# A gated FFT-and-MLP mixer on one core: first transfers regrouped, an earlier table load, two statistics on ScalarE, and a newly planned order

## Chip, core and metric

The kernel runs on one core of a Trainium2 chip. The metric is the device time of one execution in microseconds. It was timed three times: 136.17, 136.16 and 137.24 us, median 136.17. A further execution was profiled; the profile is of that one.

## What is computed

A token sequence `x` of 2048 rows by 512 columns goes through two branches, and a gate of each row mixes them:

```python
x = A_x
g = sigmoid((x * gate_w).sum(-1, keepdims=True))
# branch a: global filter in the frequency domain
X = rfft2(x.astype(float32)) * (A_w_r + 1j * A_w_i)
a = irfft2(X, s=(2048, 512)).astype(bfloat16)
# branch b: token-mixing MLP on the transposed, normalised input
h = layernorm(B_x)                                   # over the 512 columns
u = gelu(einsum("bsd,sf->bdf", h, B_w1) + B_b1)      # 2048 -> 1792
b = (einsum("bdf,fs->bds", u, B_w2) + B_b2).transpose(0, 2, 1)
return g * a + (1 - g) * b
```

The kernel reads `A_x` for both branches. Inputs and output are bfloat16.

## The kernel before, in words

**Tiling.** Row `512 q + 4 a + r` sits on partition `a`, in slot `(q, r)`, so there are 16 row tiles `j = 4 q + r` of 128 x 512. A "block" is one `r`: the four tiles `j = r, 4 + r, 8 + r, 12 + r`. Block 0 takes its tiles in the order j = 0, 8, 4, 12.

**Branch b.** VectorE (DVE) makes mean and variance of a tile (`bn_stats` L473, `bn_aggr` L474), ScalarE (ACT) the square root (L483), DVE reciprocal and -mean/std (L487, L488); the normalised tile `h` is written by ACT (L497), for j = 0, 4, 8 by DVE (L491). TensorE (PE) multiplies `h` with `w1` (L670, 14 x 16 matmuls, "m1"), ACT applies gelu (L684), PE multiplies with `w2` (L966, "m2"), ACT scales (L972) and DVE adds the other branch (L978); the last two tiles are finished by DVE alone (L984) before the stores.

**Branch a.** The 2D FFT is split into radix-4 butterflies on DVE and DFT matmuls on PE. In order: butterflies of `x` per block (L505 to L512); DFT matmuls `fa` (L524 to L527) with ACT copies L530; butterflies L537 to L544; a forward radix-4 step (`radix4`, L563 to L576) once for lt = 1 and once for lt = 0, the two halves of the frequencies, the second closed by a small copy L614; DFT matmuls `fb` (L632 to L635), eight groups for each half, each copied out by ACT (L639); column 0 is picked up by `c0a` (L754, L755) and multiplied in `c0b` (L772 to L777). Then DVE alone filters: `bfly` (L783, L784), products with the filter `W` (L791), `comb` (L796, L797), `ob` (L803 to L805), the inverse radix-4 (L563 to L579), all for lt = 0 and lt = 1. PE does the inverse DFT `i1` (L852 to L859), DVE joins (L875 to L888), PE does `i3` (L926 to L930), ACT scales by the gate (L937), DVE folds and adds (L949 to L953, L978).

**The filter's load.** `ld_W(comp)` issues 18 transfers on SyncE's (SP's) queue for the real part `A_w_r` and 18 for the imaginary part `A_w_i`, in rows of 514 bytes. `wprep` (L740, L743, L744) halves one row of `W` and adds the end columns of both parts (`wpm`, used by `c0b`). It reads both parts, so it can run only when the last filter transfers of `A_w_i` have landed.

**The order of the work.** Everything is added as a task with an engine, an estimated duration, what it reads and writes, and a priority. `Plan.order` plays the tasks through: whenever an engine is free, the ready task with the lowest priority number goes next. The emission order of the tasks is the program order of each engine, and on the chip each engine then runs strictly in that order, waiting where an input is late. So the planner's durations never cost time themselves; they only decide the order. A transfer's end is estimated from a rate (`RATE`, L132). `ld_W` is entered with 9.0 us of SP for the real part and 7.0 us for the imaginary one (L446).

**Names for the prediction's steps.** `ASTAT`, `XQ` and `here` come with the change; `PQ0` is the priority of block 0's butterflies; `HACT` the tiles normalised by ACT; `biasT`/`biasev` (L644 to L654) turn the biases to columns, which the gelu needs. PSUM has tags `fa` and `fb` with two buffers each, `acc` with four.

Of the kernel before, what the change touches and what calls it, by code (L numbers as in the profile page):

```python
# [16 lines left out]
P = 128  # L17
S = 2048
D = 512
# [109 lines left out]
    return {"flip": bf(np.eye(P)[::-1]), "ta": bf(ta), "ti": bf(ti), "tb": bf(tb), "tg": bf(tg)}  # L129


RATE = lambda t: 300e3 if t < 2.6 else 225e3 if t < 5.9 else 380e3  # L132


class Task:
# [3 lines left out]
class Plan:  # L139
# [32 lines left out]
    def order(self):  # L172
        for n, t in enumerate(self.tasks):
            t.left = len(t.deps)
            for d in t.deps:
                d.users.append(t)
        caps = dict(self.caps)
        pending = {}
        key = {t: (t.prio, n) for n, t in enumerate(self.tasks)}
        for t in self.tasks:  # L180
            if not t.left:
                pending.setdefault(t.eng, []).append(t)
        clock = {}
        dma_free = 0.0
        events = [(0.0, 0, None)]
        seq = 1
        out = []
        n_done = 0
        while events:
            now = events[0][0]  # L190
            while events and events[0][0] <= now + 1e-9:
                _, _, t = heapq.heappop(events)
                if isinstance(t, Task):
                    n_done += 1
                    for f in t.free:
                        caps[f] += 1
                    for u in t.users:
                        u.left -= 1
                        lat = self.SAME.get(u.eng, 0.0) if u.eng == t.eng else self.LAT
                        u.ready = max(u.ready, now + lat)  # L200
                        if not u.left:
                            pending.setdefault(u.eng, []).append(u)
                            heapq.heappush(events, (u.ready, seq, None))
                            seq += 1
            progress = True
            while progress:
                progress = False
                for eng, ts in pending.items():
                    if clock.get(eng, 0.0) > now + 1e-9:
                        continue  # L210
                    best = None
                    for t in ts:
                        if t.ready <= now + 1e-9 and all(caps[a] > 0 for a in t.alloc):
                            if best is None or key[t] < key[best]:
                                best = t
                    if best is None:
                        continue
                    ts.remove(best)
                    for a in best.alloc:
                        caps[a] -= 1  # L220
                    out.append((now, len(out), best))
                    clock[eng] = now + best.dur
                    end = now + best.dur
                    if best.nbytes:
                        dma_free = max(dma_free, now + best.dur + 1.0) + best.nbytes / RATE(dma_free)
                        end = dma_free + 0.9
                        clock[eng] = max(clock[eng], dma_free - 5.0)
                    best.end = end
                    heapq.heappush(events, (clock[eng], seq, None))
                    heapq.heappush(events, (end, seq + 1, best))  # L230
                    seq += 2
                    progress = True
        assert n_done == len(self.tasks), (n_done, len(self.tasks))
        self.total = max(t.end for t in self.tasks)
        return [t for _, _, t in out]
# [28 lines left out]
def kernel(  # L264
# [97 lines left out]


    Q0 = (0, 2, 1, 3)
    for r in range(4):
        if r == 0:
            for n, q in enumerate(Q0):
                ld([("x", 0, q)], lambda q=q: t["x"][:, q, 0, :], x4[:, q, 0, :], 131072, -9 + 0.1 * n, "SP" if n % 2 == 0 else "ACT")
        else:
            ld([("x", r, q) for q in range(4)], lambda r=r: t["x"][:, :, r, :], x4[:, :, r, :], 524288, 2 * r - (3 if r == 1 else 0))  # L370
        ld([("ta", r)], lambda r=r: t["ta"][:, r, :], tabs["ta"][:, r, :], 163840, 2 * r + 0.2 if r else -3.5)
# [16 lines left out]
    HI, LO, ALL = slice(P // 2, P), slice(0, P // 2), slice(0, P)  # L388
    w1_0(0, 0, LO, "ACT", -8)
    w1_0(1, 0, HI, "SP", -8)  # L390
    w1_0(0, 2, ALL, "ACT", -4)
    w1_0(0, 1, ALL, "SP", -4)
    w1_0(0, 3, ALL, "ACT", -3)
    for r in range(1, 4):
        add("SP", 0.5, ld_w1(r), writes=[("w1", 0, 4 * q + r) for q in range(4)], prio=2 * r + 0.5, nbytes=1024 * FA)
    load("flip", [P, P], BF16, tabs["flip"], 32768, prio=7)
# [57 lines left out]


    HACT = set(range(NJ)) - {0, 8, 4}
    PQ0 = 1.1
    for r in range(4):
        xk = [("x", r, q) for q in range(4)]
        groups = [[q] for q in Q0] if r == 0 else [[0, 1], [2, 3]]  # L460
        t["xf", r] = None
        for b, qs in enumerate(groups):
            js = [4 * q + r for q in qs]
# [7 lines left out]
            for j in js:  # L471
                def bn(j=j):
                    V.bn_stats(out=t["stats"][:, j, :], in_=t["x"][:, j // 4, j % 4, :])  # L473
                    V.bn_aggr(out=t["mv"][:, j, :], in_=t["stats"][:, j, :])  # L474
                add("DVE", d1(512) + 0.12, bn, reads=[("x", r, j // 4)], writes=[("mv", j)], prio=1.2 * r - (0.6 if r == 0 else 0))
# [6 lines left out]
            def sq(colv=colv, mvv=mvv):  # L482
                A.activation(colv("rstd"), mvv(1), ActF.Sqrt, bias=t["eps"][:, 0:1], scale=1.0)  # L483
            add("ACT", 0.25, sq, reads=mvk + ["eps"], writes=[("rstd", *g)], prio=-1)

            def rec(colv=colv, mvv=mvv, js=js):
                V.reciprocal(colv("rstd"), colv("rstd"))  # L487
                V.scalar_tensor_tensor(colv("nmr"), mvv(0), -1.0, colv("rstd"), op0=Alu.mult, op1=Alu.mult)  # L488
                for j in js:
                    if j not in HACT:  # L490
                        V.tensor_scalar(t["h"][:, j // 4, j % 4, :], t["x"][:, j // 4, j % 4, :], t["mv"][:, j, 0:1],  # L491
                                        t["rstd"][:, j:j + 1], op0=Alu.subtract, op1=Alu.mult)
            own = [j for j in js if j not in HACT]
            add("DVE", 0.25 + 0.32 * len(own), rec, reads=xb + mvk, writes=[("rstd", *g)] + [("h", j) for j in own], prio=1.2 * r - (0.2 if r else 0.9))
            for j in js:
                if j in HACT:
                    add("ACT", act(512, 2), lambda j=j: A.activation(t["h"][:, j // 4, j % 4, :], t["x"][:, j // 4, j % 4, :], ActF.Identity,  # L497
                                                                  bias=t["nmr"][:, j:j + 1], scale=t["rstd"][:, j:j + 1]),
                        reads=xb + [("rstd", *g)] + mvk, writes=[("h", j)], prio=-0.5 + 0.1 * r)

# [143 lines left out]
    def biasT():  # L644
        pb = t["pbias"] = ps([P, 32], F32, "fa", 2)
        T.matmul(pb[:, 0:NFT], lhsT=t["b1b"][:], rhs=t["flip"][:, P - NFT:P], start=True, stop=True)
        for r in range(4):
            T.matmul(pb[:, 16 + 4 * r:20 + 4 * r], lhsT=t["b2b"][:, r::4], rhs=t["flip"][:, P - 4:P], start=True, stop=True)
    add("PE", 0.3, biasT, reads=["bias", "flip"], writes=["pbias"], prio=9, alloc=["fa"])

    def biasev():
        V.tensor_copy(t["b1f"][:], t["pbias"][:, NFT - 1::-1])
# [20 lines left out]
    order = [(ft, j) for c in range(6) for j in jorder[2 * c:2 * c + 2] for ft in range(NF)]  # L673
    order += [(ft, j) for ft in range(NF) for j in jorder[12:]]
    order += [(ft, j) for ft in range(NF, NFT) for j in jorder]
    gelus = []
    m1t = []
    for n, (ft, j) in enumerate(order):
        last = j == jorder[-1]
        bank = bankof(ft)  # L680
        m1t.append(add("PE", mm(512), lambda ft=ft, j=j: m1(ft, j), reads=[("w1", w1of(ft), j), ("h", j)] + ([("w1", 0, j, n) for n in range(2)] if j % 4 == 0 else []), writes=[("u", ft)],
                       prio=10 + n * 1e-3, alloc=[bank] if j == jorder[0] else (), free={NF - 1: ["wa"], NF + 3: ["wb"], NFT - 1: ["wb"]}.get(ft, ()) if last else ()))
        if last:
            gelus.append(add("ACT", act(512, 1), lambda ft=ft: A.activation(  # L684
                t["gl"][:, ft, :], t["u", ft][:], ActF.Gelu_apprx_tanh, bias=t["b1f"][:, ft:ft + 1], scale=1.0),
                reads=[("u", ft), "b1f"], writes=[("gl", ft)] + ([("xf", (ft - 6) // 4)] if ft >= 6 else []), prio=0.5,
                free=[bank]))


# [1 line left out]
    for r in range(4):  # L691
# [4 lines left out]
        for q in range(4):  # L696
            def ga(q=q, r=r):
                A.activation(t["x"][:, q, r, :], t["x"][:, q, r, :], ActF.Copy, accum_out=t["glog"][:, 4 * q + r:4 * q + r + 1])  # L698
            gates.append(add("ACT", act(512) + 0.1, ga, reads=xk, writes=[("xg", q, r)], prio=5))
# [329 lines left out]
```

## Time and profile before

| | us |
|---|---|
| median of three timed runs | 136.17 |
| the profiled execution's own time | 135.25 |
| its span in the profile | 133.1 |
| PE busy | 125.3 (94% of the span) |
| DVE busy | 112.4 (84%) |
| ACT busy | 80.4 (60%) |
| first m1 matmul (L670) starts | 6.61 |
| last DVE instruction (L984) ends | 130.77 |

The granted TensorE clock is 1.0 throughout. The span is 2.15 us shorter than the execution's own time; what lies around the span is taken as unchanged. Matmuls of 128 x 512 are pipelined: one record lasts 0.38 us, but they start 0.216 us apart (28 of L670 take 6.42 us from first start to last end). Times below are from the start of the span.

### The profile page before, as it was taken

What the parts mean: (1) busy time and instruction counts of PE and PEld (TensorE: products, weight loads), DVE (VectorE), ACT (ScalarE), POOL (GpSimd) and SP (SyncE); (2) the same over time, 40 slices, a digit from 0 to 9 for tenths busy, and PEclk for the clock granted to TensorE, in tenths of its full rate; (3) what the DMA queues carried; (4) which work ended last, traced back from release to release, by engine and by line L of the source; (5) the groups of instructions that cost most, each with busy time, mean ns of one, the idle gap of its engine ahead of it and who ended that gap; (6) DMA issues with size and microseconds to landing.
All of it is one profiled execution on the core that took longest, in us unless ns stands there. A gap on an engine that the chain in (4) does not pass through costs nothing.

```text
span 133.1 us, 2156 instructions
## 1 busy us (share of the span) xinstructions
PE 125.3 (94%) x766; PEld 70.6 (53%) x780; DVE 112.4 (84%) x252; ACT 80.4 (60%) x157; POOL 0.2 (0%) x4
## 2 busy tenths in 40 slices
PE   6699899999799999999999999999999999999991
PEld 2245454545354475844445554556675665665591
DVE  2999999999969997359999999999777587979671
ACT  3344989975999999994222053332997557385500
POOL 0000000000000000000000000000000000000000
PEclk9999999999999999999999999999999999999999
DMA  4999999945499468899964800000000002130331
GB/s 148 263 381 389 395 390 385 371 88 128 92 259 285 93 152 273 271 415 402 412 246 145 330 0 0 2 5 2 0 0 0 5 0 106 52 158 5 158 118 40
DMA packets 17510, 23.18 MB, mean 174 GB/s; under 512 B 1606, under 2 KB 14940, under 8 KB 17500
## 3 DMA queue, kind: packets, MB, share of 16 engines
q1 hardware_dynamic: 16844, 22.21, 49.2%
q10 hardware_dynamic: 656, 0.84, 2.0%
q8 instruction: 6, 0.10, 0.3%
q14 instruction: 4, 0.03, 0.1%
HBM read 20.93 MB, written 2.10 MB: 173 GB/s over the span
## 4 chain that ended last, share of the span: by engine, by line
DVE 53%; PE 26%; ACT 13%; issue 4%; DMA 2%; DVEq 0%; ACTq 0%
PE acc L966 12%; DVE stats L473 7%; PE acc L670 4%; DVE xp L791 3%; DVE st L791 3%; ACT x L698 3%; ACT eo L937 3%; DVE st L564 3%; DVE mv L474 2%; DMA x<-in_A_x_dram 2%; ACT gl L684 2%; DVE xp L796 2%; DVE xp L563 2%; DVE B L803 2%; DVE xp L797 2%
## 5 line engine op out<-in xcount | busy, mean ns | idle before, releaser
L966 PE MATMUL acc<-gl,wa 128*128 128x512 bf16 (+1 forms) x107 | 26.9, 372 | 0.2
L966 PE MATMUL acc<-gl,wb 128*128 128x512 bf16 (+1 forms) x110 | 27.1, 372 | 0.1
L670 PE MATMUL acc<-h,wb 128*128 128x512 bf16 x108 | 25.7, 379 | 0.2
L972 ACT ACTIVATE x<-acc,ombb,omg 128x512 bf16<-128x512 f32 x14 | 10.8, 778 | 19.2 <-PE acc L966 19.1
L966 PEld LDWEIGHTS <-wa 128*128 128x128 bf16 x126 | 13.4, 114 | 9.8 <-issue 0.2
L966 PEld LDWEIGHTS <-wb 128*128 128x128 bf16 x126 | 13.4, 114 | 9.4
L670 PE MATMUL acc<-h,wa 128*128 128x512 bf16 x62 | 17.0, 379 | 1.5 <-DMA wa<-in_B_w_dram 1.0
L670 PEld LDWEIGHTS <-wb 128*128 128x128 bf16 x112 | 10.9, 98 | 11.7
L670 PEld LDWEIGHTS <-wa 128*128 128x128 bf16 x112 | 10.1, 98 | 10.7 <-DMA wa<-in_B_w_dram 1.8
L530 ACT CAST X<-fa 128x512 bf16<-128x512 f32 x16 | 9.3, 578 | 5.1 <-PE fa L527 5.1
L684 ACT ACTIVATE gl<-acc,b1f 128x512 bf16<-128x512 f32 x11 | 7.6, 694 | 7.8 <-PE acc L670 7.7
L473 DVE BATCH_NORM_STATS2 stats<-x 128x6 f32<-128x512 bf16 x16 | 10.8, 673 | 1.5 <-DMA x<-in_A_x_dram 1.5
L497 ACT ACTIVATE h<-x,nmr,rstd 128x512 bf16<-128x512 bf16 x13 | 10.0, 807 | 0.8 <-DVE nmr L488 0.8
L698 ACT ACTIVATE x<-x 128x512 bf16<-128x512 bf16 x16 | 10.0, 638 | 0.0
L670 PE MATMUL fb<-h,wa 128*128 128x512 bf16 x32 | 9.3, 379 | 0.1
L937 ACT ACTIVATE eo<-fa,g 128x512 bf16<-128x512 f32 x8 | 5.5, 688 | 6.1 <-DVE x L978 5.6
L355 PE MATMUL fa<-xp 128*128 128x512 bf16 x10 | 4.4, 623 | 1.2 <-DVE xp L316 1.2
L524 PE MATMUL fa<-rot,gl 128*128 128x256 bf16 x16 | 4.3, 271 | 1.2 <-ACT X L530 1.1
L937 ACT ACTIVATE eo<-fb,g 128x512 bf16<-128x512 f32 x8 | 5.5, 687 | 0.0
L670 PE MATMUL fa<-h,wa 128*128 128x512 bf16 x15 | 5.4, 379 | 0.0
L483 ACT ACTIVATE rstd<-mv,eps 128x2 f32<-128x2 f32 (+1 forms) x10 | 3.0, 295 | 3.4 <-DVE mv L474 2.8
L639 ACT CAST B<-fb 128x512 bf16<-128x512 f32 x8 | 4.9, 611 | 0.0
(172 smaller groups left out, 228.8 us busy)
## 6 DMA issues: line engine op xcount, KB each, us to landing
wb<-in_B_w_dram SPq DMA_DIRECT2D x11, 512.0 KB
wa<-in_B_w_dram SPq DMA_DIRECT2D x7, 512.0 KB
wa<-in_B_w_dram SPq DMA_DIRECT2D x3, 896.0 KB
x<-in_A_x_dram SPq DMA_DIRECT2D x3, 512.0 KB
wb<-in_B_w_dram SPq DMA_DIRECT2D x4, 384.0 KB
out_dram<-x SPq DMA_DIRECT2D x3, 512.0 KB
rot<-dft_ti SPq DMA_DIRECT2D x1, 736.5 KB
rot<-dft_ta SPq DMA_DIRECT2D x4, 160.0 KB
```

The lines of the kernel that those rows point to most:

```text
L355: T.matmul(pw[:], lhsT=t["warm"][:, 0:P], rhs=t["warm"], start=True, stop=True)
L473: V.bn_stats(out=t["stats"][:, j, :], in_=t["x"][:, j // 4, j % 4, :])
L497: add("ACT", act(512, 2), lambda j=j: A.activation(t["h"][:, j // 4, j % 4, :], t["x"][:, j // 4, j % 4, :], ActF.Identity, bias=t["nmr"][ ...
L530: add("ACT", act(512), lambda r=r, dq=dq: A.copy(t["X"][:, :, r, :, dq, :], t["pa", r, dq][:]), reads=[("pa", r, dq)], writes=[("X", r, dq ...
L639: A.copy(t["B"][:, lt, e, 2 * c:2 * c + 2, :].rearrange("p s (i b) -> p s i b", b=4), t["pb", lt, e, c][:].rearrange("p s b i -> p s i b"))
L670: T.matmul(t["u", ft][:], lhsT=w[:, j // 4, j % 4, c * P:(c + 1) * P], rhs=t["h"][:, j // 4, j % 4, :], start=(j == jorder[0]), stop=(j == ...
L684: gelus.append(add("ACT", act(512, 1), lambda ft=ft: A.activation(t["gl"][:, ft, :], t["u", ft][:], ActF.Gelu_apprx_tanh, bias=t["b1f"][:, ...
L698: A.activation(t["x"][:, q, r, :], t["x"][:, q, r, :], ActF.Copy, accum_out=t["glog"][:, 4 * q + r:4 * q + r + 1])
L791: V.tensor_mul(o, xs, w)
L937: A.activation(t["eo", j // 2][:, j % 2], t["i3", j][:], ActF.Copy, scale=t["g"][:, j:j + 1])
L966: T.matmul(t["y", j, n][:, cs], lhsT=w[:, o, 512 * q + r:512 * q + 512:4], rhs=t["gl"][:, ft, cs], start=(ft == 0), stop=(ft == NFT - 1))
L972: A.activation(tbuf(j).rearrange("p h d -> p (h d)"), t["y", j, 0][:], ActF.Identity, bias=t["ombb2"][:, j:j + 1], scale=t["omg"][:, j:j + 1])
```

## The change

The planner's transfer model gets another rate and a window of eight outstanding transfers per landing; some estimated durations are replaced; and these parts of the program change:

- Block 0 of `x` is loaded by three transfers on SP (j = 0; j = 8; j = 4 and 12 together) instead of four on SP and ACT; the first `w1` pieces (q = 0 and q = 2, 224 KB each, q = 0 no longer cut in halves) go first on ACT's queue, q = 1 and q = 3 on SP.
- Mean and variance of tiles j = 8 and j = 12 are made on ACT by two activations with accumulated sums each, into -mean and 512 x variance; the later steps of these tiles use them so.
- A tiny gelu activation (of one column) with priority 4.9, reading all `rstd`, so that the gelu table is loaded there and not at the first real gelu.
- `biasT` goes from priority 9 to -1; `PQ0` from 1.1 to -0.5.

```diff
-RATE = lambda t: 300e3 if t < 2.6 else 225e3 if t < 5.9 else 380e3
+def rate(at):
+    return 310e3 if at < 6 else 380e3
...
-                    clock[eng] = now + best.dur
-                    end = now + best.dur
+                    end = clock[eng] = now + best.dur
                     if best.nbytes:
-                        dma_free = max(dma_free, now + best.dur + 1.0) + best.nbytes / RATE(dma_free)
+                        issued = max(now, landed[-8] if len(landed) > 7 else 0.0) + best.dur
+                        clock[eng] = max(clock[eng], issued)
+                        dma_free = max(dma_free, issued + 1.0) + best.nbytes / rate(dma_free)
                         end = dma_free + 0.9
+                        landed.append(end)
...
+    XQ = ((0,), (2,), (1, 3))
...
-            for n, q in enumerate(Q0):
-                ld([("x", 0, q)], ..., 131072, -9 + 0.1 * n, "SP" if n % 2 == 0 else "ACT")
+            for n, qs in enumerate(XQ):
+                ld([("x", 0, q) for q in qs], ..., 131072 * len(qs), -9 + 0.1 * n)
...
-    w1_0(0, 0, LO, "ACT", -8)
-    w1_0(1, 0, HI, "SP", -8)
-    w1_0(0, 2, ALL, "ACT", -4)
+    w1_0(0, 0, ALL, "ACT", -8.9)
+    w1_0(0, 2, ALL, "ACT", -8.8)
     w1_0(0, 1, ALL, "SP", -4)
-    w1_0(0, 3, ALL, "ACT", -3)
+    w1_0(0, 3, ALL, "SP", -3.9)
...
-    PQ0 = 1.1
+    PQ0 = -0.5
+    ASTAT = {12, 8}
...
+                def sums(j=j):
+                    xj, junk = t["x"][:, j // 4, j % 4, :], t["h"][:, j // 4, j % 4, :]
+                    A.activation(junk, xj, ActF.Copy, scale=-1.0 / D, accum_out=t["mv"][:, j, 0:1])
+                    A.activation(junk, xj, ActF.Square, bias=t["mv"][:, j, 0:1], scale=1.0, accum_out=t["mv"][:, j, 1:2])
+                if j in ASTAT:
+                    add("ACT", 1.25, sums, reads=[("x", r, j // 4)], writes=[("mv", j), ("h", j)], prio=-0.6)
+                    continue
-                add("DVE", d1(512) + 0.12, bn, ...)
+                add("DVE", d1(512) + 0.2, bn, ...)
...
-    add("PE", 0.3, biasT, reads=["bias", "flip"], writes=["pbias"], prio=9, alloc=["fa"])
+    add("PE", 0.3, biasT, reads=["bias", "flip"], writes=["pbias"], prio=-1, alloc=["fa"])
...
+    add("ACT", 1.6, lambda: A.activation(t["ombb2"][:, 0:1], t["rstd"][:, 0:1], ActF.Gelu_apprx_tanh),
+        reads=[k for k in pl.last_w if k[0] == "rstd"], writes=["gelu"], prio=4.9)
...
-                reads=[("u", ft), "b1f"], ...
+                reads=[("u", ft), "b1f", "gelu"], ...
```

The durations of the square root (0.25 to 0.22), of L497 (to 0.71) and of the gate's activation (+0.02) are the other edits. In the compiled order `wprep` (L740, L743, L744) stands on DVE right after L576 of lt = 1 and before the forward radix-4 of lt = 0; before the change it stood behind that step, L614 and the first `c0a`. The DVE instructions from L783 to L888 keep their sequence but for three small ones (L704 to L706).

More of the change, by code (lines that the diff above doesn't have):

```diff
@@ L184, in order @@
         dma_free = 0.0
+        landed = []
         events = [(0.0, 0, None)]
@@ L364 @@
     Q0 = (0, 2, 1, 3)
+    XQ = ((0,), (2,), (1, 3))
     for r in range(4):
         if r == 0:
-            for n, q in enumerate(Q0):
-                ld([("x", 0, q)], lambda q=q: t["x"][:, q, 0, :], x4[:, q, 0, :], 131072, -9 + 0.1 * n, "SP" if n % 2 == 0 else "ACT")
+            for n, qs in enumerate(XQ):
+                ld([("x", 0, q) for q in qs], lambda qs=qs: t["x"][:, qs[0]:qs[-1] + 1:2, 0, :], x4[:, qs[0]:qs[-1] + 1:2, 0, :], 131072 * len(qs), -9 + 0.1 * n)
         else:
@@ L387, in w1_0 @@
             alloc=["wa"] if n == 0 and q == 0 else (), nbytes=2 * FA * (ps_.stop - ps_.start), after=[a0])
-    HI, LO, ALL = slice(P // 2, P), slice(0, P // 2), slice(0, P)
-    w1_0(0, 0, LO, "ACT", -8)
-    w1_0(1, 0, HI, "SP", -8)
-    w1_0(0, 2, ALL, "ACT", -4)
+    ALL = slice(0, P)
+    w1_0(0, 0, ALL, "ACT", -8.9)
+    w1_0(0, 2, ALL, "ACT", -8.8)
     w1_0(0, 1, ALL, "SP", -4)
-    w1_0(0, 3, ALL, "ACT", -3)
+    w1_0(0, 3, ALL, "SP", -3.9)
     for r in range(1, 4):
@@ L456 @@
     HACT = set(range(NJ)) - {0, 8, 4}
-    PQ0 = 1.1
+    PQ0 = -0.5
+    ASTAT = {12, 8}
     for r in range(4):
         xk = [("x", r, q) for q in range(4)]
-        groups = [[q] for q in Q0] if r == 0 else [[0, 1], [2, 3]]
+        groups = [[q] for q in Q0] if r == 0 else [[0, 1], [2], [3]] if 12 + r in ASTAT else [[0, 1], [2, 3]]
         t["xf", r] = None
@@ L474, in bn @@
                     V.bn_aggr(out=t["mv"][:, j, :], in_=t["stats"][:, j, :])
-                add("DVE", d1(512) + 0.12, bn, reads=[("x", r, j // 4)], writes=[("mv", j)], prio=1.2 * r - (0.6 if r == 0 else 0))
+                def sums(j=j):
[5 more added lines that the diff above has]
+                    continue
+                add("DVE", d1(512) + 0.2, bn, reads=[("x", r, j // 4)], writes=[("mv", j)], prio=1.2 * r - (0.6 if r == 0 else 0))
             mvk = [("mv", j) for j in js]
@@ L480, in mvv, with sq, rec @@
                 return v[:, qs[0]:qs[-1] + 1, r, c]
[L482 to L486, printed above, removed]
+            here = js[0] in ASTAT
+            def sq(colv=colv, mvv=mvv, here=here):
+                A.activation(colv("rstd"), mvv(1), ActF.Sqrt, bias=t["eps"][:, 0:1], scale=1.0 / D if here else 1.0)
+            add("ACT", 0.22, sq, reads=mvk + ["eps"], writes=[("rstd", *g)], prio=-1)
+            def rec(colv=colv, mvv=mvv, js=js, here=here):
                 V.reciprocal(colv("rstd"), colv("rstd"))
-                V.scalar_tensor_tensor(colv("nmr"), mvv(0), -1.0, colv("rstd"), op0=Alu.mult, op1=Alu.mult)
+                V.scalar_tensor_tensor(colv("nmr"), mvv(0), 1.0 if here else -1.0, colv("rstd"), op0=Alu.mult, op1=Alu.mult)
                 for j in js:
@@ L491, in rec @@
                         V.tensor_scalar(t["h"][:, j // 4, j % 4, :], t["x"][:, j // 4, j % 4, :], t["mv"][:, j, 0:1],
-                                        t["rstd"][:, j:j + 1], op0=Alu.subtract, op1=Alu.mult)
+                                        t["rstd"][:, j:j + 1], op0=Alu.add if j in ASTAT else Alu.subtract, op1=Alu.mult)
             own = [j for j in js if j not in HACT]
@@ L496 @@
                 if j in HACT:
-                    add("ACT", act(512, 2), lambda j=j: A.activation(t["h"][:, j // 4, j % 4, :], t["x"][:, j // 4, j % 4, :], ActF.Identity,
+                    add("ACT", 0.71, lambda j=j: A.activation(t["h"][:, j // 4, j % 4, :], t["x"][:, j // 4, j % 4, :], ActF.Identity,
                                                                   bias=t["nmr"][:, j:j + 1], scale=t["rstd"][:, j:j + 1]),
@@ L683 @@
         if last:
-            gelus.append(add("ACT", act(512, 1), lambda ft=ft: A.activation(
+            gelus.append(add("ACT", act(512, 1) , lambda ft=ft: A.activation(
                 t["gl"][:, ft, :], t["u", ft][:], ActF.Gelu_apprx_tanh, bias=t["b1f"][:, ft:ft + 1], scale=1.0),
-                reads=[("u", ft), "b1f"], writes=[("gl", ft)] + ([("xf", (ft - 6) // 4)] if ft >= 6 else []), prio=0.5,
+                reads=[("u", ft), "b1f", "gelu"], writes=[("gl", ft)] + ([("xf", (ft - 6) // 4)] if ft >= 6 else []), prio=0.5,
                 free=[bank]))
@@ L698, in ga @@
                 A.activation(t["x"][:, q, r, :], t["x"][:, q, r, :], ActF.Copy, accum_out=t["glog"][:, 4 * q + r:4 * q + r + 1])
-            gates.append(add("ACT", act(512) + 0.1, ga, reads=xk, writes=[("xg", q, r)], prio=5))
+            gates.append(add("ACT", act(512) + 0.12, ga, reads=xk, writes=[("xg", q, r)], prio=5))
     add("ACT", 0.3, lambda: A.activation(t["g"][:], t["glog"][:], ActF.Tanh, scale=0.5),
```

## Prediction

> **What bounds the kernel now.** I read first the page's engine table and its chain, then the chain in order of time, then the timelines of the engines around the places that the new order changes.
>
> ```profile
> PE 125.3 (94%) x766; PEld 70.6 (53%) x780; DVE 112.4 (84%) x252; ACT 80.4 (60%) x157; POOL 0.2 (0%) x4
> DVE 53%; PE 26%; ACT 13%; issue 4%; DMA 2%; DVEq 0%; ACTq 0%
> ```
>
> PE is busy longest, but more than half of the chain that ends last runs over DVE: two bounds lie close together. From L783 at 58.48 to L579 at 94.71 the chain is DVE without a real gap, and PE meanwhile fills itself with matmuls that nothing waits for. How close they lie is seen at the end of the timeline:
>
> ```profile
> 127.12 0.68 DVE L978 TENSOR_TENSOR x<-x,eo 128x1024 bf16<-128x1024 bf16 x1
> 127.72 0.74 DVE L984 SCALAR_TENSOR_TENSOR x<-acc,omg,x 128x512 bf16<-128x512 f32 x1
> 128.85 0.48 DVE L984 SCALAR_TENSOR_TENSOR x<-acc,omg,x 128x256 bf16<-128x256 f32 x1 [0.39 <-PE acc L966]
> 129.63 0.35 DVE L984 SCALAR_TENSOR_TENSOR x<-fa,omg,x 128x128 bf16<-128x128 f32 x1 [0.30 <-PE fa L966]
> 130.42 0.35 DVE L984 SCALAR_TENSOR_TENSOR x<-fb,omg,x 128x128 bf16<-128x128 f32 x1 [0.43 <-PE fb L966]
> ```
>
> DVE waits for PE there only 0.39 + 0.30 + 0.43 = 1.1 us in all. So whatever comes later than about that much on DVE comes out at the end, and what PE gains at the beginning is worth little unless DVE gains it too.
>
> Next, DVE where `wprep` was moved, and SP, which issues the filter:
>
> ```profile
> 46.44 0.69 DVE L576 TENSOR_TENSOR X<-st 128x1024 bf16<-128x1024 bf16 x1
> 47.04 1.22 DVE L563 TENSOR_TENSOR xp<-X 128x2048 bf16<-128x2048 bf16 x1
> ...
> 51.96 0.26 DVE L614 CAST X<-fx 128x32 bf16<-128x32 f32 x1
> ...
> 53.04 0.42 DVE L740 TENSOR_SCALAR W<-W 1x1028 bf16<-1x1028 bf16 x1 [0.41 <-ACT W L733]
> ...
> 58.48 1.22 DVE L783 TENSOR_TENSOR xp<-B 128x2048 bf16<-128x2048 bf16 x1
> ```
>
> ```profile
> 47.23 1.94 SPq L305 DMA_DIRECT2D W<-in_A_w_i_dram  x3
> 49.21 0.42 SPq L305 DMA_DIRECT2D wn<-in_A_w_i_dram  x1
> ```
>
> SP is still issuing the imaginary filter at 49.17; the row that L740 needs is the second of those three (issued about 47.9), and its completion events in the trace are at 51.00 and 51.23. At 53.04 nobody notices. The changed order puts L740 where L563 stands now, at 47.04.
>
> **The change, part by part.** *First transfers.* The first m1 matmul waits for `w1` (PE, 1.04 us idle before 6.61). Issued at 0.72 instead of 1.63, it comes some 0.9 earlier; the first square root no longer stands behind ACT's transfer issue at 4.21 (0.34 us). Together the first matmul comes about 1.1 us earlier, at 5.5. Neither can be seen exactly: 0 to 1.3.
>
> *Two statistics on ACT.* DVE loses 2 x (L473 + L474), 0.80 us from start to start: -1.6 us. ACT gains four activations with accumulators; L698 is the row for them, 0.61 us apart, or up to 0.72 where the next must read the sum: 2.4 to 2.9 us. ACT had 2.7 us idle before 8.67 (1.69 + 0.50 + 0.54). DVE now waits for ACT's root of j = 8 ahead of block 0's butterflies, so I count half of the 1.6.
>
> *Gelu load.* The row is 1.28 us at 32.16 and ends PE's wait of 0.91 (before 34.67) and DVE's of 1.12 (before 38.00). In the new order it stands behind the last normalisation, where ACT now idles 1.61 us: both waits go. If that idle is gone, they stay. `biasT` costs its 0.2 us on PE earlier instead of at 30.0: nothing. Durations and rates in the planner cost nothing themselves.
>
> *The order.* All of that makes DVE reach L740 sooner: at 47.04 - 1.1 - 0.8 = 45.1 or so. There it waits for SP. What of SP's queue moves? Nothing in it up to the filter waits for PE, DVE or ACT in a way that binds; it follows the transfers. These moved 554 + 548 KB in 2 to 6 us (277, 274 GB/s) and 369 GB/s in the two microseconds after; at that rate it would have been 1476 KB, so 374 KB or 1.0 us is the most that regrouping can gain. It can lose too: 448 KB of `w1` now stand on ACT's queue beside the first tile. I take a bound of -0.3 to +1.0 and the value +0.5, since the dip at 3.5 to 4.5 us (111 and 115 GB/s) falls on the first `w1` rows, which now come beside `x`. L740's input then lands at 50.7, and DVE stands still for 5 to 6 us.
>
> The Trainium skill, "DMA: Bandwidth & Descriptors", section "Issuing engines are not separate DMA queues", speaks against that +0.5: starting transfers on several engines saves only the time to issue them. By it the input stays at 51.2 and the sum below is 0.5 higher.
>
> **The sum, from L740 on**, in rows of before:
> - L740 50.8; `wprep` until the next instruction (53.04 to 53.90) 0.86: 51.65.
> - L563, L564, L568, L569 of lt = 0 (47.04 to 50.64) 3.6: 55.25. Two small copies 0.2; L575, L576 (50.64 to 51.96) 1.3; six `c0b` (53.90 to 54.55) 0.65; L614 0.26: 57.65.
> - Only then PE may start `fb` for lt = 0: 57.75, before 53.01. PE's order has 168 m1 ahead of it instead of 156 (12 x 0.216 = 2.6 us more done), yet it runs dry for some 4 us.
> - ACT's first copy 0.53 later; eight copies 0.48 apart, the last 0.60. The gelu that stood between them (57.30 instead of 56.41, 0.89 us) is gone. 57.75 + 0.53 + 3.36 + 0.60 + 0.11 = 62.35 for L783, against 58.48: +3.9.
> - From L783 through L888 the same instructions in the same order but for three small ones, dense: L888 ends 104.86 + 3.9 = 108.75, first L949 (2.03 later) at 110.8.
> - The tail: ACT and DVE take 5.38 us for two pairs (106.89 to 112.27). The new order makes three such rounds, 16.1, then fold 1.6, add 0.6, L947 0.45, fold 1.6, four L984 1.7: 22.1. Before it was 130.77 - 106.89 = 23.9. The end is 132.9.
> - PE alone: 53.01 to the last matmul's end at 130.37 is 77.4; less 2.6, from 57.75: 132.5, and its last L984 132.9. Both agree.
>
> 132.9 - 130.77 = +2.1 us. Against the profiled execution's own 135.25 that is 137.4. The median of the runs is 0.9 above that execution, so the forecast is 138.3. Of the gains ahead of 50.8 (1.1, 0.8, 1.1) nothing is left.
>
> **The rivals.** *The gains stay (faster).* If the filter lands before DVE asks, L740 to L783 takes 11.55 us from 45.1, L783 is at 56.7, and PE ends by its own gains, 1.1 + 0.9 = 2.0 earlier: 134.2. The end moves with the landing, so this needs it before 50.7 - 2.1 = 48.6. Against it: SP issues that row at 47.9. For it: a queue front that came 2.6 us sooner. 0.10.
>
> *It evens out (within 1%).* The landing comes 1.5 us or more before 51.2, or the tail's rounds are shorter than I count because more m2 is done by then: +0.8, 137.0. Against it: even the largest gain that I allow leaves 137.8, 0.3 over the line. 0.18.
>
> *The change does not do what it says:* the load not hidden, or DVE waiting longer for ACT's sums in block 0. Up to 2 us, but it all lies ahead of 50.8 and DVE has 5 us there: no change to the forecast.
>
> **How the numbers follow.** Forecast, slower by over 1%: 0.72. About 1% (1.4 us) is what a measurement of this kernel can tell from no change; the lines are 134.8 and 137.5. The forecast's own range goes with the landing, from 137.8 (SP 1.0 earlier) to 139.1 (0.3 later). Leaving out the faster rival and a little above, the range is 136.6 to 139.3. Faster 0.10, same 0.18, slower 0.72.
>
> **What would show it.** Right: a wait of 4 to 6 us on DVE before L740, put down to the filter's transfers; a PE gap of some 4 us before the second `fb`; L783 near 62; the last four L984 without much waiting; the first m1 near 5.5 and no gap of PE at 33 to 35. Wrong: L740 without a wait, or SP through with the imaginary filter before 47; or L783 at 62 and an end no later than before, which would mean that DVE had slack which I do not see.

## The result and the profile after

The changed kernel takes 142.57 us (median of 140.82, 142.72, 142.54 and 142.61) beside 136.16 for the kernel before: a ratio of 1.043, 95% interval 1.033 to 1.053. It is slower, as forecast, but by 6.4 us where 2.1 were forecast. The profiled execution took 140.82 us, its span is 139.0 us, and its mean granted clock is 0.98. Medians here and below are of all executions; ratios and intervals leave out those over 1.5% above the fastest of the same kernel. Lines of the code move by 4 to 16: L740 is now L756, L614 L628, L783 L799, L632 L646, L888 L904, L949 L965, L984 L1000.

The page's engine table and its chain, which was 53% DVE before:

```profile
PE 126.7 (91%) x766; PEld 71.7 (52%) x780; DVE 110.8 (80%) x248; ACT 84.1 (60%) x166; POOL 0.2 (0%) x4
...
PE 41%; DMA 25%; DVE 14%; SPq 12%; ACT 3%; issue 2%; DVEq 0%; ACTq 0%
```

DMA and SP's queue, 2% of the chain before, now carry 37%: the chain runs back through the filter's transfers. The timeline of DVE shows where it crosses over (in brackets: idle time ahead of the row, and what ended it):

```profile
45.31 0.68 DVE L590 TENSOR_TENSOR X<-st 128x1024 bf16<-128x1024 bf16 x1
52.47 0.42 DVE L756 TENSOR_SCALAR W<-W 1x1028 bf16<-1x1028 bf16 x1 [6.47 <-DMA W<-in_A_w_i_dram]
...
58.79 0.24 DVE L628 CAST X<-fx 128x32 bf16<-128x32 f32 x1
...
64.77 1.22 DVE L799 TENSOR_TENSOR xp<-B 128x2048 bf16<-128x2048 bf16 x1
```

The wait is where it was forecast, but it ends at 52.4 and not at 50.7. SP's queue shows the same delay:

```profile
37.73 3.06 SPq L309 DMA_DIRECT2D wt<-in_A_w_i_dram  x5
40.84 10.33 SPq L309 DMA_DIRECT2D W<-in_A_w_i_dram  x12
51.21 0.41 SPq L309 DMA_DIRECT2D wn<-in_A_w_i_dram  x1
```

The same rows before:

```profile
37.74 2.81 SPq L305 DMA_DIRECT2D wt<-in_A_w_i_dram  x5
40.60 8.57 SPq L305 DMA_DIRECT2D W<-in_A_w_i_dram  x12
```

SP begins with the imaginary filter at 37.73 (before 37.74), but its last issue is at 51.21 instead of 49.21. The timeline of PE around the two places where it waits for the filter, directly or by way of DVE:

```profile
45.58 0.38 PE L736 MATMUL fa<-wt,flip 128*128 128x256 bf16 x2 [1.90 <-DMA wt<-in_A_w_i_dram]
...
59.09 0.29 PE L646 MATMUL fa<-tb,X 128*128 128x128 bf16 x1 [3.68 <-DVE X L628]
59.17 0.31 PE L647 MATMUL fa<-tb,X 128*128 128x128 bf16 x1
59.27 0.63 PE L649 MATMUL fa<-tb,X 128*128 128x256 bf16 x2
...
62.07 0.38 PE L649 MATMUL fa<-tb,X 128*128 128x256 bf16 x2
```

The first row is a consumer that the prediction did not list: PE's flips of the imaginary filter (L736, before at 46.30 and 51.50, the second behind the fb of lt = 1) also went ahead. The L649 rows show a second surprise: the same pair of matmuls takes 0.63 us at 59.27 and 0.38 at 62.07. The stretches around them (length, busy time and instructions of PE, PEld, DVE, ACT and POOL, then the granted clock, the DMA share and GB/s):

```profile
55.40:59.09 3.69, 0.01 (x2) 0.01 (x1) 3.60 (x14) 0.83 (x4) 0.00 (x0) 0.91 0.84 311
59.09:61.80 2.71, 2.71 (x16) 2.18 (x18) 0.00 (x0) 1.75 (x3) 0.00 (x0) 0.50 1.03 416
```

PE idles 3.69 us and then runs 2.7 us at a granted clock of 0.50; in stretches of half a microsecond that clock is seen from 58.4 to 61.8. Last, DVE at the end:

```profile
134.31 1.14 DVE L1000 SCALAR_TENSOR_TENSOR x<-acc,omg,x 128x512 bf16<-128x512 f32 x2
135.37 0.34 DVE L1000 SCALAR_TENSOR_TENSOR x<-fa,omg,x 128x128 bf16<-128x128 f32 x1
135.63 0.34 DVE L1000 SCALAR_TENSOR_TENSOR x<-fb,omg,x 128x128 bf16<-128x128 f32 x1
```

It no longer waits for PE there; the end is 135.97, 5.2 us after the 130.77 of before.

### The profile page after: what moved, and what is told of

It reads as the page before. It is cut to its first block, busy times and chain, and to the rows that moved or that the text cites. A ratio compares the mean times of both kernels' runs of the same rounds, so it can differ in the third digit from the quotient of the medians.

```text
span 139.0 us, 2156 instructions
## 1 busy us (share of the span) xinstructions
PE 126.7 (91%) x766; PEld 71.7 (52%) x780; DVE 110.8 (80%) x248; ACT 84.1 (60%) x166; POOL 0.2 (0%) x4
## 3 DMA queue, kind: packets, MB, share of 16 engines
q1 hardware_dynamic: 17180, 22.59, 47.6%
## 4 chain that ended last, share of the span: by engine, by line
PE 41%; DMA 25%; DVE 14%; SPq 12%; ACT 3%; issue 2%; DVEq 0%; ACTq 0%
PE acc L982 24%; SPq L309 12%; DMA wa<-in_B_w_dram 9%; PE acc L684 8%; DMA wt<-in_A_w_i_dram 5%; DMA wb<-in_B_w_dram 5%; DMA W<-in_A_w_r_dram 3%; ACT eo L953 3%; DMA W<-in_A_w_i_dram 2%; DVE eo L968 2%; DVE es L967 2%; DVE x L994 1%; PE fa L868 1%; DVE es L966 1%; PE fb L868 1%
## 5 line engine op out<-in xcount | busy, mean ns | idle before, releaser
L684 PE MATMUL acc<-h,wb 128*128 128x512 bf16 x108 | 25.1, 379 | 0.2
L988 ACT ACTIVATE x<-acc,ombb,omg 128x512 bf16<-128x512 f32 x14 | 10.8, 780 | 19.0 <-PE acc L982 19.0
L684 PE MATMUL acc<-h,wa 128*128 128x512 bf16 x61 | 17.6, 393 | 0.3
L478 DVE BATCH_NORM_STATS2 stats<-x 128x6 f32<-128x512 bf16 x14 | 9.4, 675 | 2.0 <-DMA x<-in_A_x_dram 2.0
L653 ACT CAST B<-fa 128x512 bf16<-128x512 f32 x8 | 4.9, 615 | 3.8 <-PE fa L649 3.7
L684 PE MATMUL fa<-h,wa 128*128 128x512 bf16 x16 | 5.9, 379 | 0.0
L965 DVE COPY es<-eo 128x8 bf16<-128x8 bf16 x8 | 1.5, 188 | 5.3 <-ACT eo L953 4.9
L756 DVE TENSOR_SCALAR W<-W 1x1028 bf16<-1x1028 bf16 x1 | 0.4, 421 | 6.5 <-DMA W<-in_A_w_i_dram 6.5
```

The source lines that it names most:

```text
L653: A.copy(t["B"][:, lt, e, 2 * c:2 * c + 2, :].rearrange("p s (i b) -> p s i b", b=4), t["pb", lt, e, c][:].rearrange("p s b i -> p s i b"))
L684: T.matmul(t["u", ft][:], lhsT=w[:, j // 4, j % 4, c * P:(c + 1) * P], rhs=t["h"][:, j // 4, j % 4, :], start=(j == jorder[0]), stop=(j == ...
L988: A.activation(tbuf(j).rearrange("p h d -> p (h d)"), t["y", j, 0][:], ActF.Identity, bias=t["ombb2"][:, j:j + 1], scale=t["omg"][:, j:j + 1])
```

## The experiments

Theory 1: the loss comes from work that the new order puts ahead of the imaginary filter's landing. The rival: it comes from the transfers, ACT's added work or the rest of the order.

| kernel | median us | ratio to the kernel before | 95% interval |
|---|---|---|---|
| e1, wprep moved back | 136.39 | 1.000 | 0.996 to 1.004 |
| e2, filter issued first | 135.02 | 0.989 | 0.982 to 0.997 |
| e3, 16 filler matmuls | 141.03 | 1.030 | 1.023 to 1.037 |
| e4, before, one planner figure | 142.47 | 1.036 | 1.025 to 1.046 |
| e6, changed kernel again | 141.53 | 1.032 | 1.024 to 1.040 |
| e7, as e3 | 140.75 | 1.023 | 1.014 to 1.032 |
| e8, before, filter first | 136.29 | 1.002 | 0.998 to 1.006 |
| e9, after, one planner figure | 135.31 | 0.990 | 0.987 to 0.994 |
| e10, filter first, planned so | 133.68 | 0.980 | 0.975 to 0.985 |
| e11, e2 without early load | 135.05 | 0.992 | 0.989 to 0.996 |
| e12, e2 with old transfers | 135.76 | 0.997 | 0.994 to 1.000 |
| e13, fillers at both waits | 140.46 | 1.032 | 1.027 to 1.037 |
| e14, changed kernel again | 142.01 | 1.040 | 1.034 to 1.046 |
| e15, e10 without ASTAT | 134.73 | 0.990 | 0.986 to 0.994 |

e1 to e4, e5 to e8, e9 to e12 and e13 to e15 each shared their runs of the kernel before (medians 136.25, 135.87, 135.83, 136.12). e5 is a profile of the kernel before: 136.82 us.

**e1: wprep alone back.** The planned list of tasks is edited by hand:

```diff
-    order_ = pl.order()
+    order_ = pl.order(); wp = [t_ for t_ in order_ if t_.emit.__name__ == "wprep"][0]; order_.remove(wp); order_.insert(order_.index([t_ for t_ in order_ if t_.emit.__name__ == "c0b"][0]), wp)
```

> The changed kernel with the three wprep instructions alone moved back behind the forward radix-4 of lt = 0, L628 and the first c0a; every other instruction keeps its place. Theory 1 (the wait of 6.47 us for the imaginary filter's row is the whole loss): DVE begins that radix-4 at 46.0, L628 ends near 51.7 instead of 59.03, fb of lt = 0 starts near 51.8 (before the change 53.01), PE does not run dry there and the granted clock is 1.0 until the last matmul, L799 starts near 57.3 (before 58.48) and the time is 1 to 2 us under the kernel before: 134 to 135.5. Rival (the loss lies in the rest of the new order, in the regrouped transfers or in ACT's added work, and the wait covers it): the time stays above 138.

The loss is gone, but the time is that of the kernel before and not 1 to 2 us under it. DVE in e1:

```profile
49.10 0.68 DVE L583 TENSOR_TENSOR X<-xp 128x1024 bf16<-128x1024 bf16 x1
53.16 0.17 DVE L770 CAST c<-B 128x8 f32<-128x8 bf16 x1 [3.37 <-ACT B L653]
...
56.34 0.24 DVE L628 CAST X<-fx 128x32 bf16<-128x32 f32 x1
```

L628 is at 56.3 and not near 51.5. A small part is that `wprep`, put ahead of `c0b`, still stands ahead of L628, which comes last in the changed order (0.85 us). The larger part: c0a (L770) waits for ACT's copies of lt = 1. These stand behind ACT's copy of the flipped filter (L740, 3.03 us idle ahead of it), and that behind PE:

```profile
46.97 0.38 PE L736 MATMUL fa<-wt,flip 128*128 128x256 bf16 x2 [3.12 <-DMA wt<-in_A_w_i_dram]
```

So the new order has two early consumers of the filter, wprep on DVE and the flips on PE. While wprep waited longest, it hid the other.

**e2: the landing moved instead.** DVE, PE and ACT keep their order, wprep too:

```diff
-    order_ = pl.order()
+    order_ = pl.order(); order_.remove(t["ldW", 1]); order_.insert(order_.index(t["ldwb", 1, 0]), t["ldW", 1])
```

> The changed kernel with the 18 transfers of the imaginary filter issued on SP ahead of the four w1 pieces (4 x 384 KB) that stand before them; DVE, PE and ACT keep their order, wprep too. Theory 1: the row that L756 waits for is issued about 2.7 us earlier (four issues of 0.65) and without the waits of 2.0 and 0.6 us behind those pieces, so it lands near 47 instead of 52.4; the wait before L756 falls from 6.47 to 1 us or less, L799 from 64.77 to about 59, and the time to 134 to 136.5. The end moves with the landing until DVE no longer waits. Rival (the place of wprep in the order costs by itself, landing or not): over 138 with no wait before L756.

DVE in e2:

```profile
45.62 0.69 DVE L590 TENSOR_TENSOR X<-st 128x1024 bf16<-128x1024 bf16 x1
47.76 0.42 DVE L756 TENSOR_SCALAR W<-W 1x1028 bf16<-1x1028 bf16 x1 [1.45 <-ACT B L653]
```

The wait falls from 6.47 to 1.45 us, a little over the 1 expected, L799 starts at 59.05, and the time is 135.02: the place of wprep costs little once the row is there. (The ACT instruction named is not what ended that wait: ACT's L749, which wprep also needs, ends at 45.56; the chain has a filter transfer landing at 47.6.)

**e3 and e7: the clock, first try.** Inside the first fb of lt = 0, ahead of its matmuls:

```diff
-                    pb = t["pb", lt, e, c] = ps([P, 2, 4, 64], F32, tag, 2)
+                    pb = t["pb", lt, e, c] = ps([P, 2, 4, 64], F32, tag, 2); [T.matmul(pb[:].rearrange("p s b i -> p (s b i)"), lhsT=t["flip"][:], rhs=t["tb"][:, 0:512], start=True, stop=True) for _ in range(16 if (lt, e, c) == (0, 0, 0) else 0)]
```

> The changed kernel with 16 matmuls of 128x512 on constant tables put into PE's order right before the first fb of lt = 0; they write the bank that this fb then overwrites. They take 16 x 0.216 = 3.5 us and fit into the idle 3.7 us. Wait, landing and order stay. Theory 1a (beside the wait itself, the half clock granted from 58.4 to 61.8 costs): the clock is 1.0 at 59 to 62, the eight fb groups run at full speed, and the time falls by 0.7 to 1.5 us, more in the executions with a lower mean clock. Rival (fb is paced by ACT's copies 0.48 us apart, so PE's clock costs nothing there): within 0.4 us of the changed kernel, 142.2 to 143.

> The kernel of e3 again, beside the changed kernel on the same chip, because the first profile of it was disturbed. Theory 1a (the half clock behind the idle stretch costs beside the wait): 0.7 to 2 us under the changed kernel, granted clock 1.0 at 59 to 62 of the profile. Rival (fb is paced by ACT's copies): within 0.4 us of it.

e7 is 0.8 us under e6 on the same chip, but the intervals overlap, and the profile of e7 is no clean case: PE's wait for the flips was 4.06 us there, the clock was 0.5 from 46.9 to 53.7 already, and the fillers then began so late (60.41) that fb started at 63.86, 2.5 us after L628 had ended. Nothing is decided by these two. e3's profile, of an execution of 194.9 us at a mean clock of 0.66, is not used.

**e4: the order alone, in the kernel before.**

```diff
-        add("SP", 9.0 - 2 * comp, ld_W(comp), ...
+        add("SP", 9.0 - 4 * comp, ld_W(comp), ...
```

> The kernel before with one planner figure changed, the SP time of the imaginary filter 5.0 instead of 7.0 us: no instruction is added or removed and no transfer moves, only the order is planned anew, with wprep ahead of the forward radix-4 of lt = 0 as in the changed kernel. Theory 1: DVE stops at L740 from about 47.0 until the row lands at 51.0 to 51.2, a wait of 4 us; fb of lt = 0 starts at 57 instead of 53.01, PE runs dry, the clock drops to one half for a window, and the time is 3 to 5 us over the kernel before: 139 to 141. Rival (the loss comes from the transfers, the statistics or the table load of the change and not from the order): 135.5 to 137.

DVE in e4:

```profile
46.65 0.69 DVE L576 TENSOR_TENSOR X<-st 128x1024 bf16<-128x1024 bf16 x1
53.41 0.42 DVE L740 TENSOR_SCALAR W<-W 1x1028 bf16<-1x1028 bf16 x1 [6.07 <-ACT B L639]
```

One figure in the planner, with no instruction or transfer added, makes the kernel before 6.2 us slower by the medians; its ratio, 1.036, has the 1.043 of the whole change inside its interval. The median is 1.5 us over the expected range: L740 starts at 53.41, where the row was expected at 51.0 to 51.2. (Here too the ACT row named is not what ended the wait: ACT's L733, the copy that wprep needs, ends at 47.74, and the trace has a filter transfer's completion at 53.30 and 53.33.)

**e5, e6 and e14: does the landing vary?**

> The kernel before, unchanged, for a second profile. It is to tell why the imaginary filter landed at 52.4 in the changed kernel where 50.7 was forecast, with SP's last filter issue (wn) at 51.21 instead of 49.21. If the landing varies from execution to execution, wn is issued at some other time than 49.2 here too, by a microsecond or more, and the time stays near 136 because nothing waits for it. If the regrouped first transfers make the landing late, wn is again at 49.2, within 0.4.

> The changed kernel, unchanged, for a second profile and as the measure for the filler on the same chip: 141.5 to 143. If the landing varies by itself, the row that L756 waits for lands at another time than 52.4 and the profiled execution's own time goes with it, about 1 us for 1 us; if it is fixed by the program, the landing is 52.4 and the time that of the first profile.

> The changed kernel again, as the measure for e13 and for a third profile: 141 to 143 with the landing anywhere from 51 to 55.

SP in e5, the kernel before in a second execution:

```profile
38.36 2.92 SPq L305 DMA_DIRECT2D wt<-in_A_w_i_dram  x5
41.33 9.77 SPq L305 DMA_DIRECT2D W<-in_A_w_i_dram  x12
51.15 0.42 SPq L305 DMA_DIRECT2D wn<-in_A_w_i_dram  x1
```

The last issue is 1.9 us later than in the first profile of the same program. The other profiles with the filter behind the four w1 pieces have it at 51.21 (after), 52.68 (e1), 52.06 (e4), 52.77 (e6), 53.43 (e7), 50.55 (e13), 51.75 (e14) and, in an order planned anew, 49.29 (e9). The 49.21 that the prediction rests on is the earliest of these ten. Two parts make up most of the spread. SP waits in the middle of the filter for the w1 pieces ahead of it to land, 1.9 us in the first profile before and in e9, 2.6 in the first after, and up to 3.2 (e1, e4). And in after, e1, e4, e6, e7 and e14 one issue takes 1.45 to 2.05 us, its neighbours 0.43. DVE in e6, the changed kernel in a second execution of 142.91 us:

```profile
45.61 0.69 DVE L590 TENSOR_TENSOR X<-st 128x1024 bf16<-128x1024 bf16 x1
54.21 0.42 DVE L756 TENSOR_SCALAR W<-W 1x1028 bf16<-1x1028 bf16 x1 [7.92 <-ACT B L653]
```

The wait ends 1.74 us later than in the first profile, and the time is 2.09 us longer (as in e2, the ACT row named had ended; SP issued wn at 52.77). The other 0.33 us lie between the first fb of lt = 0 and L799, 6.01 us instead of 5.68, more of it at the half clock (see e13). In e14 the row comes 0.71 us later than in the first profile, that stretch takes 7.12 us, 1.44 more, and the time is 2.16 longer. In the changed kernel the end follows the landing and the clock behind it; the kernel before did not notice the landing.

**e8: the same transfers in the kernel before** (e2's edit on the other kernel).

> The kernel before with the 18 transfers of the imaginary filter issued ahead of the four w1 pieces, as in e2. In the kernel before nothing waits for that filter (L740 at 53.04, its row in at 51.2). Theory 1: the time is that of the kernel before within 0.5 us, and the 1.2 us that e2 gained are the change's own gains (earlier first m1, table load, statistics). Rival (the new transfer order is what gained in e2): 134.5 to 135.3.

No change, as theory 1 has it. So e2's 1.2 us are not gains of the transfer order by itself, but of the change.

**e9: the planner told the truth.** In the changed kernel:

```diff
-        add("SP", 9.0 - 2 * comp, ld_W(comp), ...
+        add("SP", 12.7 - 0.8 * comp, ld_W(comp), ...
```

> The changed kernel with one planner figure changed, the SP time of the two filter loads 12.7 and 11.9 us (measured in the kernel before) instead of 9.0 and 7.0: no instruction and no transfer is added or removed, the order is planned anew. In it wprep stands on DVE behind L800 of lt = 0, and PE's flips of the imaginary filter (L736, L746) stand behind the fb of lt = 1. Theory 1 (what costs is every consumer of the imaginary filter that is placed ahead of its landing: DVE's wprep and PE's flips): no wait of over 0.5 us for that filter on PE or DVE, granted clock 1.0 throughout, and the time is 0.5 to 1.5 us under the kernel before. Rival (the gains ahead are only worth something with the filter issued first): equal to the kernel before, within 0.4 us.

135.31 us, 0.5 under the kernel before (ratio 0.990, 0.987 to 0.994): with the measured length of two tasks the change is a small gain instead of a loss, though single executions reach from 134.4 to 137.5. The profile has no wait for the filter on PE or DVE.

**e10: filter first, and the planner told of it.**

```diff
-        add("SP", 9.0 - 2 * comp, ld_W(comp), ..., prio=17 + 8 * comp, ...
+        add("SP", 13.2 - 3 * comp, ld_W(comp), ..., prio=17 + 2 * comp, ...
```

> The changed kernel with the imaginary filter issued ahead of the four w1 pieces, and the planner told of it (priority 19 instead of 25, SP times 13.2 and 10.2 us). wprep then stands behind L583 of lt = 0, L628 comes near 52.2 (in e2 at 54.1). Theory 1: PE's last wait ahead of fb (0.74 us in e2) goes; the time is 0.3 to 0.8 us under e2: 134.2 to 134.8. Rival (PE and DVE are balanced in the tail, so nothing comes of it): within 0.3 us of e2's 135.0.

133.68 us, 2.0% under the kernel before (1.5 to 2.5%), more than expected. DVE in e10, at the end:

```profile
127.17 1.18 DVE L1000 SCALAR_TENSOR_TENSOR x<-acc,omg,x 128x512 bf16<-128x512 f32 x2
128.65 0.35 DVE L1000 SCALAR_TENSOR_TENSOR x<-fa,omg,x 128x128 bf16<-128x128 f32 x1 [0.30 <-PE fa L982]
129.43 0.35 DVE L1000 SCALAR_TENSOR_TENSOR x<-fb,omg,x 128x128 bf16<-128x128 f32 x1 [0.43 <-PE fb L982]
```

DVE waits for PE again: PE is the bound here, busy for 95% of the span. This version beats both kernels.

**e11, e12 and e15: what the parts are worth.** e11 leaves the early gelu out of e2, e12 gives e2 the old first transfers, e15 sets `ASTAT = set()` in e10; each is planned anew.

> e2's kernel without the early gelu activation, so that the gelu table is loaded at the first real gelu again. The prediction's step was that this load made PE wait 0.91 us and DVE 1.12. Theory 1: with the filter's wait out of the way that gain reaches the end, and without the early load the time is 0.5 to 1.0 us over e2: 135.5 to 136.0. Rival (the gain is swallowed on the way, or the load is hidden anyway in this order): within 0.3 us of e2.

> e2's kernel with block 0 of x and the first w1 pieces loaded as in the kernel before (four x transfers on SP and ACT, w1 of q = 0 in two halves). First m1 near 6.6 instead of 5.8. Theory 1: that 0.8 us of PE's time reaches the end: 135.5 to 136.0. Rival (the regrouping is worth nothing at the end, DVE starts no earlier by it): within 0.3 us of e2.

> e10's kernel with all statistics on DVE again (ASTAT empty; the order is planned anew). Theory 1 (the term is worth something where no wait swallows it, half of DVE's 1.6 us at most): 0.3 to 0.8 us over e10's 133.7. Rival (PE bounds the end, DVE's 1.6 us are worth nothing): within 0.3 us of e10.

The early table load is worth nothing that these runs can tell (135.05 beside 135.02, where e2's interval is 2 us wide). The regrouped transfers may be worth 0.7 us, but the intervals overlap (the first m1 starts at 7.87 in e12 and at 6.30 in e2). The statistics on ACT are worth about 1 us: the intervals of e10 and e15 do not meet. As the orders differ too, that is the worth of the part with the order that it brings.

**e13: the clock, second try.** 8 fillers ahead of the flips, 12 ahead of fb:

```diff
-                    pw = t["pw", comp, lt, a] = ps([P, 2, L], F32, tag, 2)
+                    pw = t["pw", comp, lt, a] = ps([P, 2, L], F32, tag, 2); [T.matmul(pw[:].rearrange("p i l -> p (i l)"), lhsT=t["flip"][:], rhs=t["tb"][:, 0:512], start=True, stop=True) for _ in range(8 if (comp, a) == (1, 0) else 0)]
...
-                    pb = t["pb", lt, e, c] = ps([P, 2, 4, 64], F32, tag, 2)
+                    pb = t["pb", lt, e, c] = ps([P, 2, 4, 64], F32, tag, 2); [T.matmul(pb[:].rearrange("p s b i -> p (s b i)"), lhsT=t["flip"][:], rhs=t["tb"][:, 0:512], start=True, stop=True) for _ in range(12 if (lt, e, c) == (0, 0, 0) else 0)]
```

> The changed kernel with 8 matmuls of 128x512 on constant tables ahead of PE's flips of the imaginary filter (1.7 us, into a wait of 1.9 to 2.7 us in the two profiles of the changed kernel) and 12 ahead of fb of lt = 0 (2.6 us, into one of 3.7 and 2.6 us). Waits, landing and order stay. Theory 1a (the half clock behind each idle stretch is a part of the loss of its own): the granted clock stays 1.0 until the end of the matmuls and the time is 1 to 2.5 us under the changed kernel on the same chip. Rival (the clock costs nothing, fb is paced by ACT's copies): within 0.4 us of it, or above by what the fillers delay.

The median is 1.55 us under that of e14, the changed kernel on the same chip, and 0.9 under it without the execution of e14 that its ratio leaves out. The intervals touch, so the times alone do not decide. But in the profile of e13 the row landed when it did in the first profile after (L756 starts at 52.42 and 52.47). DVE in e13:

```profile
52.42 0.42 DVE L756 TENSOR_SCALAR W<-W 1x1028 bf16<-1x1028 bf16 x1 [5.76 <-DMA W<-in_A_w_i_dram]
...
58.74 0.24 DVE L628 CAST X<-fx 128x32 bf16<-128x32 f32 x1
...
63.71 1.22 DVE L799 TENSOR_TENSOR xp<-B 128x2048 bf16<-128x2048 bf16 x1
```

and its stretch at fb, with the granted clock as third number from the end:

```profile
59.04:62.34 3.30, 3.30 (x36) 2.77 (x36) 0.00 (x0) 2.76 (x6) 0.00 (x0) 1.00 1.03 418
```

The wait ends at the same time and fb starts at the same time (59.04 and 59.09), at full clock. From there to L799 it takes 4.67 us instead of 5.68. So the half clock behind the idle stretch is a loss of its own, 1.0 us in this pair, and the fillers pay for themselves even though they compute nothing. The other profiles of this order agree: 4.67 us in e2 at full clock, 6.01 in e6 and 7.12 in e14, where more of the stretch ran at 0.50. The profiled execution takes 139.44 us instead of 140.82; of the other 0.3 us, which are gained behind L799 at full clock in both, no cause is shown.

## Why the prediction was right in direction and 4 us short

The mechanism was right: DVE waits for the filter, PE runs dry behind it, and the end moves. What failed is the size of two of its terms, the landing and the stretch from fb to L783, and the way from the profile to the median. The sum was 132.9 for the end of the last L984; it is 135.97. Step by step:

- **The wait: right.** DVE stands at L756 for 6.47 us (5 to 6 forecast), put down to the filter's transfers. e1, e2, e4 and e9 show from four sides that work placed ahead of the landing makes the loss, and of the gains ahead of it nothing is left.
- **The landing: failed.** "I take a bound of -0.3 to +1.0 and the value +0.5" was to put it at 50.7. It is 52.4, +1.67 us on the sum. The term was SP's gain from the regrouping. There is none: SP starts the imaginary filter at 37.73 and 37.74, and in the later profiles with this transfer order not earlier (37.92 to 39.05 with the first transfers regrouped, 38.36 and 38.51 without). On that point the rule of the Trainium skill, "DMA: Bandwidth & Descriptors", section "Issuing engines are not separate DMA queues", held. But the bound stood on one completion time of one execution, and that moves: SP's last issue was 49.2 to 53.4 in ten executions with this transfer order. In the first profile after, 0.7 us of its delay are the longer wait for the w1 pieces and 1.1 us the one long issue. A queue that nobody waits for had been read to a tenth of a microsecond.
- **wprep to L628: right.** 6.85 us forecast, 6.56 measured. PE's dry stretch: some 4 us forecast, 3.69 measured.
- **From fb to L783: failed.** The "eight copies 0.48 apart" were taken from rows at full clock: 4.60 us. Measured 5.68, +1.08: the first four copies are 0.64 apart, as PE ran at 0.50. e13, with the clock at 1.0, takes 4.67 us. The step that named PE's dry stretch did not ask what the clock does behind it.
- **L799 to the last L904: right.** 46.40 forecast, 46.32 measured. The stretch is not "dense", though: DVE waits there for ACT, 2.06 us in all, but it did so before as well (2.36 us), and the forecast carried that along in its rows.
- **The tail: nearly right.** The three rounds take 16.10 us, 16.1 forecast. 2.57 us instead of 2.05 from L904 to the first L965, where ACT waits for PE at L988 ahead of the first pair's scaling; from there to the end 22.31 against 22.1. Together +0.73.
- **Around the span: +0.37.** From the last L984 to the execution's own time it was 4.48 us before, now 4.85.
- The landing, fb, the tail, the span's surroundings and the smaller differences (-0.29, -0.04, -0.08) give 3.44; measured were 140.82 - 137.4 = 3.42.
- **Profile to median: failed.** 0.9 was added as before; it is 1.75. The profiled execution is the fastest of the four, with one half-clock stretch and a mean clock of 0.980; the other three, which were only timed, have 0.973 or 0.974. e6, 142.91 us, had a landing at 54.2 and two such stretches. That the timed ones were like it is likely, not shown.
- **The front: too hopeful, without effect.** First m1 at 5.79 (6.28 in e6), not 5.5; DVE reaches L756 at 46.0, not 45.1. The first statistics start later, 3.78 instead of 3.32 (4.27 and 4.22 in e6 and e14).
- **The gelu load: right as a mechanism, empty as a gain.** Both waits are gone (L551 starts at 37.90 without one); e11 shows nothing of it at the end.
- **Not listed at all:** the flips of the imaginary filter on PE. In the first profile their 1.90 us lay beside DVE's longer wait; e1, in which they alone still wait for the filter, has nothing left of the 1.2 us that e2 gains.

Of the rivals, "the gains stay" needed the landing before 48.6: e2 makes just that by moving the transfers, and gains 1.2 us of the 2.0 that the rival counted. Why the w1 pieces land later in one execution than in another was not settled.

## What to carry to other kernels

Before an operation is moved ahead of a transfer's landing, read that landing from more than one execution: a queue with slack shows only one sample of a wide spread, and the planner's own figure for it (7.0 us against 11.9 measured) is no measurement. List every consumer of what the planner believes to be early, on all engines, because the longest wait hides the others. And where a wait leaves PE dry for some 3 us, add the half clock that may follow to the sum, here about 1 us in the first profile, or fill the stretch.

## What was not expected of the hardware

The clock behind an idle stretch of PE. It fell to one half behind idle stretches of 2.64 and 2.74 us (e6), 3.69 (after), 3.98 (e4), 4.06 (e7) and 4.48 (e14), and did not behind 1.59 (e14), 1.90 (after) and 3.12 us (e1). It stayed there for 3.4 us at a time, or for twice that: in e14 the mean clock from 59.8 to 65.9 was 0.53. In the second profile of the changed kernel (e6) two such stretches:

```profile
47.70:51.10 3.40, 3.40 (x17) 1.95 (x16) 0.00 (x0) 2.65 (x8) 0.00 (x0) 0.50 0.43 93
61.10:64.60 3.50, 3.50 (x23) 2.44 (x21) 0.00 (x0) 2.64 (x5) 0.00 (x0) 0.54 1.02 412
```

The Trainium skill, "TensorE: Matmul & The Clock Gate", section "Part 1: The HAM clock gate (the "warmup" mystery)", describes half rate after at least one idle window of about 3.4 us, with windows that run freely. The length of the half-rate stretches agrees (3.4 us), and so does the different effect of like idle times (3.12 us without, 2.74 with). But an idle stretch of 2.64 us is shorter than such a window and was enough here.

One issue on SP of the filter took 1.55 us where its neighbours took 0.43 (at 47.21 in the first profile after; 1.51 at 46.85 in e14; 1.45 to 2.05 in e1, e4, e6 and e7). In each of these six profiles a 16 KB transfer on the instruction queue (q8 on the page) starts within 0.4 us of that issue's start. In before, e5, e9 and e13, where no issue of the filter is that long, it starts earlier, at 43.39, 45.29, 41.72 and 41.25. A wait for instructions would fit that, but nothing was run to test it.
